# Bias rows written in three DMAs, their tails laid out by GpSimd, and a planner with a shorter cold time

## The chip, the cores and the metric

The kernel runs on one core of one Trainium2 chip. The metric is device time in microseconds (us) of one execution, and the median of several. All times of rows are from one execution recorded by the hardware profiler, counted from its first instruction.

## What is computed

Causal attention with a bias from cumulative sums, whose output is the input of a mixture of experts with dense gates, whose output goes through a two-layer network. The change touches the attention alone:

```python
# q, k, v: (4, 8, 576, 64), s: (4, 8, 576)
scores = scale * np.matmul(q, k.transpose(0, 1, 3, 2))
cum = np.cumsum(np.maximum(s, 0.0), axis=-1)
bias = -(cum[:, :, :, None] - cum[:, :, None, :])
scores = np.where(causal, -1000000000.0, scores + np.minimum(bias, 0.0))
scores = scores - np.max(scores, axis=-1, keepdims=True)
attn = np.exp(scores)
attn = attn / (np.sum(attn, axis=-1, keepdims=True) + 1e-09)
return np.matmul(attn, v).astype(np.float32)
```

Then x is (2304, 512); the mixture has 8 experts of 512 x 1024 x 512, the last network is 512 x 2048 x 512.

## The kernel before

**The attention.** The 32 heads are taken as 16 pairs p = 0 to 15, two heads (h = 0, 1) on the two halves of the 128 partitions. A pair has nine chunks of 128 query rows: four for each head (scores 128, 256, 384 and 512 wide) and a ninth that holds the last 64 rows of both heads (two parts, each 288 wide). For each pair:

- q, k and v are loaded into RB (q and k) and RV (`load_raw`, L403), two DMAs each, one for each head. RB has two places for q and two for k, so pair p's load waits until pair p - 2 has been transposed.
- TensorE transposes q and k (`t_pe`, L477, five each) into a PSUM tile qk, which q and k use in turn. ScalarE and VectorE round q into a high and a low part (L482 to L501, or by way of QF on GpSimd, L506 to L512). k is copied to KF (L515), and GpSimd makes its parts (L519, L533). One copy of each half of q (L490, L492) and of k (L529) goes from SBUF to SBUF by DMA (tile WQ); all of these operands lie in WQ.
- The bias enters as extra rows of the second matmul: `load_bias` (L459, L460) reads the sums of a pair from the DRAM tiles bqd and bkd. For pair 0 they come from SBUF directly.
- A score block is one matmul of the high parts (L543) and one that holds low parts and bias (L544; L548 and L549 for the ninth chunk), into the two banks sc. VectorE masks and takes the maximum (L558, L564, L569), ScalarE the exponential (L576), TensorE transposes (L613, L615) into the two banks tr, ScalarE or VectorE copies these out (L629), and two products with v (`pv0`, `pv1`, L641) fill the tile o. The sums are turned by TensorE (L588), copied (L591), sent through DRAM (L594, L598) and GpSimd scales X by them (L603, L606).

**The bias rows.** The sums over the 32 heads are made once: relu and scan on VectorE (L434, L437), rounding on ScalarE (L440) and remainder on VectorE (L443), into RS0 (64 rows: two parts, two heads of a pair, 16 pairs; 576 columns). `bias_zero` writes zeros to the 64 columns of bqd that a head doesn't use (two DMAs, L447); `bias_write` writes columns 0 to 511 (L450), the 64 tail columns in four pieces whose place depends on the head (L453), and bkd (L454).

**What sets the order.** All of it is put down as tasks (`add`) with an engine, a key, a planned duration and predecessors, and `Plan.order` lays them out: it steps through planned time and gives each engine, among the tasks that are ready, the one of the smallest key. TensorE's durations count twice before a planned time of "cold" thousand ns. The order that comes out is the program; on the chip an engine then runs its own queue strictly in that order and waits by semaphores. So planned durations and predecessors that no data needs change only the order. SP's queue is one of the engines: an issue that waits holds all issues behind it. The first product of the mixture (FA, FB and sc, L314 to L316) and its weights are planned into the end of the attention as well; all that follows has a planner of its own (`flow`).

## Time and profile before

| | us |
|---|---|
| median of 3 runs | 2034.17 (2033.29 to 2038.76) |
| profiled execution | 2032.67 |
| its span, first to last instruction | 2030.8 |
| TensorE busy in the span | 2001.0 (99%) |
| GpSimd, VectorE, ScalarE busy | 1671.3, 1652.8, 904.3 |

The attention takes about the first 210 us of the span. Busy shares are averages over all stages; a stage is read from windows of time, from what each engine waited for, and from the instructions in order of time. A row of the timeline begins with the start and the duration of a group of like instructions; a bracket at its end is the idle time before it and what ended that. SPq rows are DMA issues, whose duration is that of the issue alone.

### The profile page before, as it was taken

How to read it: one execution, taken by the hardware profiler on the slowest of the kernel's cores; microseconds unless marked ns; L12 is line 12 of the kernel's file. 1: busy time of each engine (PE TensorE's matmuls, PEld its weight loads, DVE VectorE, ACT ScalarE, POOL GpSimd, SP SyncE). 2: the span in 40 equal slices, each digit the busy share in tenths (PEclk: the TensorE clock that was granted, in tenths of full speed). 3: DMA queues.
4: the chain of work that ended last, by engine and by line, in shares of the span. 5: the costliest groups of instructions: out<-in, count | busy, mean ns of one | idle time of the engine just before them, and what ended most of it. 6: DMA issues, size and time to landing. Idle time of an engine off the chain costs nothing. (4 is left out here: it accounts for less than half of the span.)

```text
span 2030.8 us, 35314 instructions
## 1 busy us (share of the span) xinstructions
PE 2001.0 (99%) x11939; PEld 1898.0 (93%) x11939; DVE 1652.8 (81%) x2954; ACT 904.3 (45%) x1886; POOL 1671.3 (82%) x1532
## 2 busy tenths in 40 slices
PE   7999999999999999999999999999999999999999
PEld 6777798888889899999999999999999999999999
DVE  5878488888898878888988998989988885766845
ACT  5888433333333344333333344443334345555552
POOL 5778878888888768888887899888878999798783
PEclk9999999999999999999999999999999999999999
DMA  7884888888988777777777788989989877776663
GB/s 160 189 181 120 301 281 291 308 307 300 318 304 308 264 256 253 248 256 247 240 252 250 226 289 302 321 294 309 306 297 308 280 245 242 229 253 216 220 233 116
DMA packets 310241, 524.04 MB, mean 258 GB/s; under 512 B 84044, under 2 KB 197006, under 8 KB 294702
## 3 DMA queue, kind: packets, MB, share of 16 engines
q1 hardware_dynamic: 310024, 521.72, 78.3%
q8 instruction: 95, 1.56, 0.3%
q14 instruction: 84, 0.69, 0.1%
q10 hardware_dynamic: 38, 0.08, 0.0%
HBM read 367.33 MB, written 144.66 MB: 252 GB/s over the span
## 5 line engine op out<-in xcount | busy, mean ns | idle before, releaser
L314 PE MATMUL sc<-XO,WQ 128*128 128x384 f32 x960 | 323.6, 337 | 2.4 <-DVE Uu L1063 1.2
L315 PE MATMUL sc<-XO,WQ 128*128 128x384 f32 x960 | 321.6, 335 | 0.0
L316 PE MATMUL sc<-XO,WQ 128*128 128x384 f32 x960 | 321.5, 335 | 0.0
L1356 ACT CAST WQ<-WQ 128x512 fp32r<-128x512 f32 x172 | 106.9, 622 | 225.4 <-DMA WQ<-w2s 199.9
L1357 DVE TENSOR_TENSOR WQ<-WQ 128x512 fp32r<-128x512 f32 x172 | 183.5, 1068 | 29.1 <-ACT WQ L1356 28.9
L314 PEld LDWEIGHTS sc<-XO,WQ 128*128 128x128 f32 x960 | 180.4, 188 | 9.0 <-DVE Uu L1063 2.1
L315 PEld LDWEIGHTS sc<-XO,WQ 128*128 128x128 f32 x960 | 180.5, 188 | 4.3
L316 PEld LDWEIGHTS sc<-XO,WQ 128*128 128x128 f32 x960 | 180.2, 188 | 0.0
L1063 DVE TENSOR_TENSOR sc<-sc,Uu 128x384 f32<-128x384 f32 x240 | 133.9, 558 | 46.6 <-PE sc L316 45.7
L230 POOL TENSOR_TENSOR WQ<-RB,WQ 128x512 fp32r<-128x512 f32 (+1 forms) x64 | 117.4, 1843 | 58.9 <-ACT WQ L249 54.6
L314 PE MATMUL FA<-XO,WQ 128*128 128x384 f32 x480 | 162.0, 338 | 1.7 <-DVE HB L1091 1.7
L316 PE MATMUL FA<-XO,WQ 128*128 128x384 f32 x480 | 161.1, 336 | 0.3 <-POOL WQ L230 0.3
L315 PE MATMUL FA<-XO,WQ 128*128 128x384 f32 x480 | 161.0, 335 | 0.0
L1337 POOL TENSOR_TENSOR HB<-GG,HB 128x384 fp32r<-128x384 f32 x96 | 110.9, 1158 | 31.0 <-ACT HB L1336 26.3
L1378 DVE TENSOR_TENSOR X<-tr,X 128x384 f32<-128x384 f32 x212 | 115.8, 549 | 23.9 <-PE tr L1372 23.4
L1063 DVE TENSOR_TENSOR Uu<-FB,Up 128x384 f32<-128x384 f32 x120 | 66.2, 551 | 48.0 <-PE FB L316 24.9
L1143 PE MATMUL tr<-WQ,HB 128*128 128x512 f32 x256 | 101.4, 396 | 0.0
L1142 PE MATMUL tr<-WQ,HB 128*128 128x512 f32 x256 | 101.0, 394 | 0.0
L1141 PE MATMUL tr<-WQ,HB 128*128 128x512 f32 x256 | 100.0, 391 | 0.0
L1337 POOL TENSOR_TENSOR HB<-XT,HB 128x384 fp32r<-128x384 f32 x79 | 89.0, 1127 | 12.6 <-ACT HB L1336 12.4
L1063 DVE TENSOR_TENSOR Uu<-sc,Uu 128x384 f32<-128x384 f32 x120 | 65.9, 550 | 39.7 <-PE sc L316 39.4
L314 PEld LDWEIGHTS FA<-XO,WQ 128*128 128x128 f32 x480 | 90.4, 188 | 5.5 <-DVE HB L1091 2.0
(556 smaller groups left out, 7065.6 us busy)
## 6 DMA issues: line engine op xcount, KB each, us to landing
WQ<-w1c SPq DMA_DIRECT2D x88, 1024.0 KB
WQ<-w2d SPq DMA_DIRECT2D x132, 512.0 KB
WQ<-w1c SPq DMA_DIRECT2D x264, 256.0 KB
w1c<-WQ SPq DMA_DIRECT2D x32, 1792.0 KB
WQ<-w2s SPq DMA_DIRECT2D x172, 256.0 KB
RAW<-in_moe_w_dram SPq DMA_DIRECT2D x32, 512.0 KB
w2d<-WQ SPq DMA_DIRECT2D x64, 256.0 KB
w2s<-SS SPq DMA_DIRECT2D x32, 512.0 KB
```

The source lines that it names most:

```text
L230: return lambda: nc.gpsimd.tensor_tensor(out=out, in0=x, in1=y, op=op)
L314: nc.tensor.matmul(t, lhsT=hi, rhs=xh, start=new, stop=False, skip_group_check=on)
L315: nc.tensor.matmul(t, lhsT=hi, rhs=xl, start=False, stop=False, skip_group_check=on)
L316: nc.tensor.matmul(t, lhsT=lo, rhs=xh, start=False, stop=(k == 1), skip_group_check=on)
L1063: TT = lambda out, x, y: (lambda: v.tensor_tensor(out=out, in0=x, in1=y, op=ALU.add))
L1141: nc.tensor.matmul(y, lhsT=hh, rhs=wb[0][:, f], start=(f == 0), stop=False)
L1142: nc.tensor.matmul(y, lhsT=hh, rhs=wb[1][:, f], start=False, stop=False)
L1143: nc.tensor.matmul(y, lhsT=hl, rhs=wb[0][:, f], start=False, stop=(f == 1))
L1337: do(eng, t + 0.02, pgg(W) if eng == "pool" else pq(W), lambda: (nc.gpsimd if eng == "pool" else nc.vector).tensor_tensor(out=OP[k][:, 1], ...
L1356: do("act", t, pa(512), lambda: nc.scalar.copy(hi, lo.bitcast(F32)), [("w2l", k)], [("w2h", k)])
L1357: do(eng, t + 0.05, pgg(512) if eng == "pool" else pd(512), lambda: (nc.gpsimd if eng == "pool" else nc.vector).tensor_tensor(out=lo, in0= ...
L1378: do("dve", t + 0.08, pq(W), lambda: nc.vector.tensor_tensor(out=a, in0=y[:, 0:W], in1=a, op=ALU.add), [yr], [("A", name, s_)])
```

## The change

The tails come from four `affine_select` on GpSimd, which lay the 64 tail columns and the 64 zero columns of each part and head side by side in the second half of a pair's RS1 tile, so that one DMA of 64 x 128 writes them. The zero writes are gone, and bqd is written in two DMAs instead of seven. The third pair's q and k loads no longer have the load of pair 1's v as a predecessor. "cold" goes from 28 to 19, TensorE's planned durations are multiplied by 1.033, and the products with v of the first two pairs have the copies of all nine chunks as predecessors. Lines behind the new function move down by 3. The instructions after the attention come in the same order on every engine.

```diff
-KEYS = {"NE": 11, "PB": 2, "L": 26.0, "bias": 12.3, "Tq": -1.3, "Tk": 6.1, "Tev": -14.1, "Th": 7.8, "top": 17.9, "exp": 14.0, "R": 17.7, "X": 3.9, "hi": -7.3, "lo": 13.7, "cp": "ddaadaaaaddd", "cq": "ddaaddaaaddd", "seq": "012345678", "last": "162308754", "pv": 14.0, "pvh": 33.4, "o": -10.8, "cold": 28.0, "grp": 2, "QP": 1, "w2": 6.0, "w1": 6.0}
+KEYS = {"NE": 11, "PB": 2, "L": 26.0, "bias": 12.3, "Tq": -1.3, "Tk": 6.1, "Tev": -14.1, "Th": 7.8, "top": 17.9, "exp": 14.0, "R": 17.7, "X": 3.9, "hi": -7.3, "lo": 13.7, "cp": "ddaadaaaaddd", "cq": "ddaaddaaaddd", "seq": "012345678", "last": "162308754", "pv": 14.0, "pvh": 33.4, "o": -10.8, "cold": 19, "grp": 2, "QP": 1, "w2": 6.0, "w1": 6.0}
...
-        def bias_zero():
-            for h in range(2):
-                nc.sync.dma_start(out=bqd[:, h, :, S - 64 * h:640 - 64 * h].rearrange("r p n -> p r n"), in_=mask[0:16, 0:128].rearrange("p (r n) -> p r n", r=2))
+        def bias_tail():
+            BT = RS[1][0:64, 0:128]
+            for r in range(2):
+                mine = slice(32 * r, 32 * r + 32)
+                for h in range(2):
+                    nc.gpsimd.affine_select(out=BT[mine, 64 * h:64 * h + 64], in_=BKf[mine, 512:S], pattern=[[0, 64]], compare_op=ALU.is_ge, fill=0.0,
+                                            base=15 - 31 * h, channel_multiplier=2 * h - 1)
 
         def bias_write():
-            nc.sync.dma_start(out=bqd.rearrange("r h p n -> (r h p) n")[:, 0:512], in_=BKf[:, 0:512])
-            for r in range(2):
-                for h in range(2):
-                    nc.sync.dma_start(out=bqd[r, h, :, 512 + 64 * h:S + 64 * h], in_=BKf[32 * r + 16 * h:32 * r + 16 * h + 16, 512:S])
+            rows = bqd.rearrange("r h p n -> (r h p) n")
+            nc.sync.dma_start(out=rows[:, 0:512], in_=BKf[:, 0:512])
+            nc.sync.dma_start(out=rows[:, 512:640], in_=RS[1][0:64, 0:128])
             nc.sync.dma_start(out=bkd.rearrange("r h p n -> (r h p) n"), in_=BKf)
...
-            d[name] = plan.add(eng, key, dur, fn, (), lat)
+            d[name] = plan.add(eng, key, dur * (1.033 if eng == "pe" else 1), fn, (), lat)
...
-        add(("bz",), "sp", -4, 1000, bias_zero, [("setc",), ("bias", 0, 1)], DMA)
-        add(("bw",), "sp", -4, 2500, bias_write, [("cum",), ("bias", 0, 1), ("L", "q", 1)], DMA)
+        add(("bz",), "pool", -25, 1200, bias_tail, [("cum",)])
+        add(("bw",), "sp", -9, 1650, bias_write, [("cum",), ("bz",), ("bias", 0, 1), ("L", "q", 1)], DMA)
...
-                    add(("L", w, p), "sp", b9 - KEY["L"], 950, lambda raw=raw, src=src, p=p: load_raw(raw[p % 2], src, p), [("T", w, p - 2)] + [("L", x, 1) for x in "qkv"], DMA)
+                    add(("L", w, p), "sp", b9 - KEY["L"], 950, lambda raw=raw, src=src, p=p: load_raw(raw[p % 2], src, p), [("T", w, p - 2)] + [("L", x, 1) for x in "qk"], DMA)
...
-                deps = [("cp", b9 + c, a) for c in at_ for a in range(2)] + [("L", "v", p), ("xc", p - 1)] + [("pv0", p, 0)] * part
+                deps = [("cp", b9 + c, a) for c in (range(9) if p < 2 else at_) for a in range(2)] + [("L", "v", p), ("xc", p - 1)] + [("pv0", p, 0)] * part
```

**SP's queue, from the bias tails to the k copy of pair 1.** In_q, in_k and in_v are the loads, RV_100 is v of pair 0, RV_101 v of pair 1; the q and k loads behind v are those of pairs 2 and 3. L490 and L492 (L493 and L495 in the changed kernel) copy q, L529 (L532) copies k. Before:

```order
L453 DMA bqd<-RS_116 16x64 x4
L454 DMA bkd<-RS_116 64x576
L403 DMA RV_100<-in_v_dram 128x5x64 x2
L490 DMA WQ<-WQ 64x576
L403 DMA RV_101<-in_v_dram 128x5x64 x2
L459 DMA WQ<-bqd 2x2x640
L460 DMA WQ<-bkd 2x2x576
L492 DMA WQ<-WQ 64x640
L403 DMA RB<-in_q_dram 128x5x64 x2
L403 DMA RB<-in_k_dram 128x5x64 x2
L529 DMA WQ<-WQ 64x576
```

Now:

```order
L456 DMA bqd<-RS_124 64x128
L457 DMA bkd<-RS_116 64x576
L403 DMA RV_100<-in_v_dram 128x5x64 x2
L403 DMA RB<-in_q_dram 128x5x64 x2
L403 DMA RB<-in_k_dram 128x5x64 x2
L493 DMA WQ<-WQ 64x576
L462 DMA WQ<-bqd 2x2x640
L463 DMA WQ<-bkd 2x2x576
L403 DMA RV_101<-in_v_dram 128x5x64 x2
L403 DMA RB<-in_q_dram 128x5x64 x2
L403 DMA RB<-in_k_dram 128x5x64 x2
L532 DMA WQ<-WQ 64x576
```

The third pair's loads have moved ahead of the q copy and of pair 1's v; the fourth pair's loads, which stood behind the k copy, stand ahead of it, and one q copy has moved behind it.

**TensorE, from pair 0's last transposes into pair 1's scores.** L613 (L616) are transposes of the exponentials, L477 (L480) those of q and k of pair 2, L543 and L544 (L546 and L547) score blocks of pair 1. Before:

```order
L613 MATMUL tr<-ident,EB 128x128 x5
L477 MATMUL qk<-ident,RB 128x128 x5
L613 MATMUL tr<-ident,EB 128x128 x4
L543 MATMUL sc<-WQ 128x128
L544 MATMUL sc<-WQ 128x128
L543 MATMUL sc<-WQ 128x256
L544 MATMUL sc<-WQ 128x256
L613 MATMUL tr<-ident,EAB 128x128 x4
```

Now:

```order
L616 MATMUL tr<-ident,EB 128x128 x2
L480 MATMUL qk<-ident,RB 128x128 x5
L616 MATMUL tr<-ident,EB 128x128 x7
L480 MATMUL qk<-ident,RB 128x128 x5
L616 MATMUL tr<-ident,EAB 128x128 x4
L546 MATMUL sc<-WQ 128x128
L547 MATMUL sc<-WQ 128x128
L546 MATMUL sc<-WQ 128x256
L547 MATMUL sc<-WQ 128x256
```

The q transposes stand three transposes earlier, the k transposes have moved ahead of pair 1's scores, and so has the ninth chunk (EAB).

**TensorE, at the end of the attention.** L314 to L316 into sc are the last product planned ahead of the mixture, L588 (L591) turns the sums, L641 (L644) is the last pair's product. Before:

```order
L316 MATMUL sc<-XO,WQ 128x384
L613 MATMUL tr<-ident,EB 128x128 x3
L588 MATMUL o<-ident,RC 10x128
L314 MATMUL sc<-XO,WQ 128x384
L315 MATMUL sc<-XO,WQ 128x384
L316 MATMUL sc<-XO,WQ 128x384
L314 MATMUL sc<-XO,WQ 128x384
L315 MATMUL sc<-XO,WQ 128x384
L316 MATMUL sc<-XO,WQ 128x384
L641 MATMUL o<-PA_105,RV_101 64x256 x2
```

Now:

```order
L316 MATMUL sc<-XO,WQ 128x384
L616 MATMUL tr<-ident,EB 128x128 x6
L591 MATMUL o<-ident,RC 10x128
L616 MATMUL tr<-ident,EB 128x128
L644 MATMUL o<-PA_105,RV_101 64x256 x2
```

The last transposes and the turning of the sums have moved from between the products to directly ahead of the attention product.

## Rows read from the trace of the kernel before

**Rows 1.** 10 us windows: start:end, length, busy PE, PEld, DVE, ACT, POOL; clock, DMA, GB/s.

```profile
20.00:30.00 10.00, 5.35 (x31) 4.43 (x31) 4.35 (x16) 4.56 (x11) 4.12 (x4) 0.84 0.98 207
...
50.00:60.00 10.00, 10.00 (x82) 7.78 (x82) 8.15 (x30) 8.10 (x23) 7.70 (x11) 1.00 0.76 160
...
220.00:230.00 10.00, 10.00 (x56) 7.32 (x55) 2.66 (x6) 3.92 (x9) 9.24 (x11) 0.93 0.94 343
```

**Rows 2.** TensorE's waits of 0 to 230 us: total, times, longest.

```profile
PE qk L477 <- DMA RB<-in_q_dram: 6.0, 2, 4.3
...
PE sc L544 <- DMA WQ<-WQ: 1.0, 2, 0.6
```

**Rows 3.** The timeline of TensorE around its longest wait.

```profile
20.48 0.74 PE L477 MATMUL qk<-ident,RB 128*128 128x128 f32 x5
...
22.28 0.83 PE L613 MATMUL tr<-ident,EB 128*128 128x128 f32 x5
...
27.45 1.30 PE L477 MATMUL qk<-ident,RB 128*128 128x128 f32 x5 [4.33 <-DMA RB<-in_q_dram]
...
30.00 0.45 PE L544 MATMUL sc<-WQ 68*128 68x128 f32 x1 [0.30 <-issue]
...
36.30 0.44 PE L613 MATMUL tr<-ident,EB 128*128 128x128 f32 x2
```

**Rows 4.** 2 us windows over the same place.

```profile
26.00:28.00 2.00, 0.55 (x3) 0.58 (x4) 0.00 (x0) 0.00 (x0) 0.72 (x1) 0.70 1.14 261
...
30.00:32.00 2.00, 2.00 (x9) 2.00 (x10) 1.64 (x7) 0.86 (x4) 1.32 (x2) 0.50 1.34 228
32.00:34.00 2.00, 2.00 (x10) 1.79 (x9) 0.92 (x3) 1.53 (x5) 0.94 (x1) 0.60 0.50 102
```

**Rows 5.** The timeline of SP's queue: bias writes, v and pair 2's q, k copy, pair 3.

```profile
14.34 0.99 SPq L447 DMA_DIRECT2D bqd<-mask  x2
...
15.37 0.48 SPq L450 DMA_DIRECT2D bqd<-RS  x1
...
15.90 1.98 SPq L453 DMA_DIRECT2D bqd<-RS  x4
...
18.43 1.21 SPq L403 DMA_DIRECT2D RV<-in_v_dram  x2
...
23.68 1.16 SPq L403 DMA_DIRECT2D RB<-in_q_dram  x2
...
26.08 0.52 SPq L529 DMA_DIRECT2D WQ<-WQ  x1
26.70 1.20 SPq L403 DMA_DIRECT2D RB<-in_q_dram  x2
...
29.45 0.56 SPq L529 DMA_DIRECT2D WQ<-WQ  x1
```

**Rows 6.** The timeline of ScalarE and VectorE: the parts of pair 2's q.

```profile
28.83 0.64 ACT L482 ACTIVATE WQ<-qk 64x576 fp32r<-64x576 f32 x1 [4.07 <-issue]
...
30.37 0.75 DVE L498 SCALAR_TENSOR_TENSOR WQ<-qk,WQ 64x576 fp32r<-64x576 f32 x1
```

**Rows 7.** The timeline of TensorE at pair 2's first score block.

```profile
41.31 0.33 PE L544 MATMUL sc<-WQ 68*128 68x128 f32 x1 [0.60 <-DMA WQ<-WQ]
```

**Rows 8.** The timeline: a copy out of tr, and the turning of sums near the end.

```profile
22.17 0.28 DVE L629 COPY PA<-tr 128x128 f32<-128x128 f32 x1
...
194.45 0.28 PE L588 MATMUL o<-ident,RC 128*10 128x128 f32 x1 [0.72 <-DVE RC L585]
```

**Rows 9.** GpSimd and VectorE at the start; last, line 430's two selects (min/median/max).

```profile
6.37 1.34 DVE L437 TENSOR_TENSOR_SCAN EAB<-EB,EAB 32x576 f32<-32x576 f32 x1
...
8.52 0.75 DVE L443 TENSOR_TENSOR RS<-EAB,RS 32x576 fp32r<-32x576 f32 x1
...
10.93 0.67 POOL L519 TENSOR_SCALAR WQ<-KF 64x576 fp32r<-64x576 f32 x1 [2.90 <-DVE KF L515]
...
L430 POOL TENSOR_SCALAR_AFFINE_SELECT mask<-mask x2: 237/688/1138, 6.6 to 7.8; 64x64 f32<-64x64 f32 x2
```

## The prediction

> **What bounds the kernel now.** I read the 10 us windows first. In them TensorE is the engine without gaps: it is busy for all 10 us of 50 to 60, as in most windows of the attention up to 180, and again from 220 to the end [rows 1]. Nothing after the attention is reordered by this change, and TensorE has no idle time there to absorb a later or an earlier start, so the question is only when the attention hands over, and that depends on TensorE's gaps between 0 and 210 us. Second, TensorE's own waits of that stretch: one stands out, for the q rows of a pair, 4.3 us long; besides the first loads there is little else, among it two waits of 1.0 us in all for copies made by DMA (tile WQ) [rows 2]. Third, the timeline around the long wait: TensorE finishes five transposes at 22.28 + 0.83 = 23.11 and starts the q transposes of the third pair (p = 2) only at 27.45, 4.33 us later [rows 3]. Fourth, 2 us windows over the same place: the granted clock falls to one half from about 26.8 (0.70 over 26 to 28 is 1.2 us at 0.5) to about 33.6 (0.60 over 32 to 34), so 2.4 GHz became 1.2 GHz right after that idle time [rows 4]. Last, SP's queue, which issues nearly all DMAs, back to back from 14.34 to 30: the q load that TensorE waits for is issued at 23.68, behind six small bias DMAs that the change removes or merges, and behind the v loads [rows 5].
>
> **SP's queue.** Removed are the two zero writes (0.99) and the four tail writes (1.98); one tail write comes instead, taken at the 0.48 of the main write, so 2.5 us less [rows 5]. The first v load moves from 18.43 to 15.9. The third pair's q and k loads now follow it directly, so q is issued at 15.9 + 1.3 = 17.2 and not 23.68. From issue to use it took 27.45 - 23.68 = 3.8 us [rows 3, 5]: it lands at 21.0, at most 22 with the bias writes and v just ahead of it. TensorE gets there two transposes into the former five, about 22.6. **The 4.33 us wait goes.**
>
> **What is late next.** TensorE then wants the third pair's k transposes, whose PSUM tile is the one q occupies. The q transposes take 0.74 and end at 23.35, ScalarE's rounding 0.64 and VectorE's remainder 0.75 follow [rows 3, 6]: with some 0.2 us for each hand-over TensorE may go on at 25.4, idling about 1 us after the seven transposes put in between. The k transposes (0.74), those of pair 0's last chunk and half a score block bring it to an estimated 27.4. That is the first score block of pair 1, whose second matmul needs the DMA copy of k (source line 529 of the kernel before). It is issued at 26.08 and its matmul starts at 30.00, 3.92 us later [rows 3, 5]; so before the change this wait was hidden right behind the q wait. In the new order the copy stands behind the third and the fourth pair's q and k loads and both v loads. From the first v load to the copy is 26.08 - 18.43 = 7.65 us of queue; one issue leaves it (the q copy, taken at the 0.56 of the k copy and a gap), and the fourth pair's two loads come in front (29.45 - 26.70 = 2.75) [rows 5]. So it is issued at 15.9 + 7.65 - 0.6 + 2.75 = 25.7, only 0.4 us earlier than before, and with 3.92 its matmul starts at 29.6. The bounds for issue to use: 3.1, what the second half of the q load had (issued 0.6 after 23.68), and 5.3, if one more load ahead of it than before costs its transfer (327 680 bytes at the 228 to 261 GB/s that such windows show [rows 4] are 1.4 us). I take 3.92, the same kind of copy in the same crowd; the ends give 28.8 and 31.0.
>
> The Trainium skill (DMA: Bandwidth & Descriptors, "Queues, rings and completion order") says that each DMA engine consumes descriptors in ring order, which speaks against this change: the copy cannot pass the loads now put ahead of it. By that rule the 3.92 or more stands; were the copy able to pass them, 3.1 would be nearer and the sum 0.8 us better. The 3.92 of the copy, against 3.8 for a load issued before it, agrees with the rule.
>
> **From there on.** From that matmul to the first transposes behind the attention product of pair 0 the old kernel takes 36.30 - 30.00 = 6.30 us, 3.6 of them at half clock [rows 3, 4]. The new order has nearly the same instructions there. At full clock the 3.6 would be 1.8 if all of it were TensorE's own work, 6.30 - 1.8 = 4.5 in all; the chain through VectorE that frees the score banks does not halve, so I take 4.7, between 4.5 and 6.3. TensorE reaches that point at 29.6 + 4.7 = 34.3 instead of 36.30: **2.0 us gained**. Both ends together: 28.8 + 4.5 = 33.3 (3.0 gained) and 31.0 + 6.3 = 37.3 (1.0 lost).
>
> **The rest of the attention.** The 1.033 on TensorE's planned durations and the cold time of 19 change no instruction, only the order. Between 37 and 180 TensorE waits twice, 0.60 at 41.31 and 0.45 later, both for such copies [rows 2, 7]. In the new order the two k copies stand ahead of the two reads of the reciprocals; I count the 0.60 as **gained**, with 0 and 1.05 as the ends. The remaining order costs nothing as long as TensorE stays full, which it does there [rows 1]; if that cover is gone, the price is one wait of 0.45 to 0.60 per pair. That the first two pairs' products wait for all nine chunks also costs nothing: in both orders pair 0's product stands behind the last transposes of that pair and two score blocks more, longer than a copy; if that cover is gone, one copy of 0.28 and two hand-overs, 0.7 for each of the two.
>
> At the end, the last transposes of the last pair move behind the two products of the next stage, directly ahead of the attention product. That product must now wait for their copy out of PSUM: 0.28 [rows 8] and two hand-overs of some 0.2 are 0.7 lost, with 0 and 0.8 as ends. The transpose of the sums moves behind one score block and so loses some 0.3 of its wait of 0.72 [rows 8], with 0 and 0.5 as ends. Net **0.4 lost**.
>
> On GpSimd four selects on 32 x 64 are added. GpSimd is idle for 2.90 us before 10.93, waiting for k; the cumulative sums are ready at 8.52 + 0.75 = 9.27, and a 64 x 64 select takes 0.237 when undisturbed [rows 9]. Four with gaps are 1.1 us, from 9.5 to 10.6: hidden, with 0.3 us to spare.
>
> **Sum:** -2.0 - 0.6 + 0.4 = -2.2 us. The profiled execution took 2032.67 us (span 2030.8), so 2030.5; the median of the runs, 2034.17, stands 1.5 above the profiled one, so **2032.0** on that scale. The ends, -3.0 - 1.05 - 0.5 = -4.5 and +1.0 + 0.8 = +1.8, give 2029.7 to 2036.0 for this case. About 0.3% (6.1 us) is what a measurement of this kernel can tell from no change.
>
> **Rivals.**
> A. *The k copy is in time.* If it overtakes the loads and lands by 27, when its scores are due, the next point is reached near 27.0 + 4.7 = 31.7, 4.6 gained; with both copy waits (1.05) and the 0.72 gone and nothing lost at the end, -6.4 or a little more: about 2027.5. For it: the loads ahead of it start 6 us sooner. Against it: DMA is at 0.98 over 20 to 30 [rows 1].
> B. *The clock falls again.* TensorE still idles about 1 us at 24.4 and about 2 us at 27.4. It fell after the 4.33 us of idling, and I cannot read from two levels whether 3 us in pieces suffice. If it falls over the same stretch, 6.3 and not 4.7 is paid: only 0.4 of the 2.0 remain. If it falls over a stretch as long (6.8 us) where TensorE is full, 3.4 is lost against the sum: +1.2. Between 2032.6 and 2035.4; I take 2034.
> C. *Slower: the selects hold GpSimd.* One select of the old kernel took 1.138 instead of 0.237, beside VectorE's scan at 6.37 [rows 9]. Four such are 4.55, to 14.0 and not 10.6, so that the k rounding at 10.93 starts 3.1 late; it decides from 1.4 us in all on. SP's copy of that k, and all issues behind it, shift by 3.1: pair 1's k copy to 28.8, its matmul to 32.7, and after so much idling 6.3 at half clock follow: 39.0 instead of 36.3, with the end +3.1, and up to 3 more if the clock first rises later. 2037 to 2040, say 2038. Against it: at 9.5 VectorE has turned to reading PSUM. The Trainium skill (GPSIMD Engine Reference, "1. Specifications") states that the SBUF interfaces are shared with VectorE and contended by its instructions with two SBUF inputs, which fits the scan and not the two instructions that follow the sums; by it this rival is less likely, and the trace has one select of each kind.
>
> **Chances.** Forecast 0.50, A 0.17, B 0.25, C 0.08. Faster by over 0.3% means under 2028.1: A and a sliver of the forecast, 0.18. Slower means over 2040.3: the upper end of C and orders that cost a wait per pair, 0.07. The same: 0.75. The range leaves out half of A and most of C: 2026.5 to 2037.5.
>
> **What would show it.** The q transposes of pair 2 start near 22.6 without a long wait; the largest wait of TensorE between 20 and 40 is for tile WQ, about 2 us, at its first score block of pair 1 near 29.6; the clock is 1.0 over 28 to 34; the transposes after the first product start near 34.3; the attention's end comes 2 us earlier, and the later stages are as long as before. No such wait, or a stretch of half clock, or selects of over 1 us, show A, B or C; a wait at every pair between 50 and 180 would prove the whole account wrong.

## The result and the profile after

The changed kernel takes **2046.93 us** (median of six runs, 2043.74 to 2048.87) against 2034.79 of six runs of the kernel before: a ratio of **1.0054**, 95% interval 1.0042 to 1.0066, 11 us slower by the ratio (12.1 by the medians), where I forecast 2032.0 and a range up to 2037.5. The profiled execution took 2045.89, its span is 2044.1; against 2030.8 before that is 13.3 us, and the account below is made on these two spans. In the changed kernel the k copy is L532, the write of the reciprocals (the inverted sums of the softmax) to DRAM L597, its reads L601, and GpSimd's scaling of X by them, which the planner calls x_norm, L606.

10 us windows of the changed kernel (the view of [rows 1]):

```profile
30.00:40.00 10.00, 9.88 (x49) 6.89 (x50) 5.08 (x19) 5.01 (x16) 4.15 (x4) 0.66 0.67 159
...
100.00:110.00 10.00, 10.00 (x69) 7.98 (x70) 6.37 (x23) 5.46 (x16) 7.30 (x9) 0.83 1.09 216
...
200.00:210.00 10.00, 6.44 (x30) 4.81 (x27) 4.52 (x14) 5.29 (x14) 9.74 (x10) 0.71 0.00 0
...
220.00:230.00 10.00, 8.60 (x65) 5.82 (x66) 5.28 (x10) 5.05 (x10) 3.48 (x6) 1.00 0.58 176
```

The clock, which was low over 26.8 to 33.6 before, is low at three places now: 0.66 over 30 to 40 takes 3.4 us of full speed away, 0.83 over 100 to 110 takes 1.7, 0.71 over 200 to 210 takes 2.9. The 0.93 that 220 to 230 had before [rows 1] is gone. TensorE's waits between 0 and 230 us (the view of [rows 2]):

```profile
PE sc L547 <- DMA WQ<-WQ: 9.0, 8, 3.4
...
PE sc L546 <- DVE mx L561: 2.7, 2, 1.9
...
PE qk L480 <- DMA RB<-in_q_dram: 1.1, 1, 1.1
```

The long wait for q is gone: 1.1 us in place of 6.0. The waits for the copies of k went from 1.0 us in two to 9.0 in eight. Where the time went can be read from the start of each pair's product with v (first row of tile PA) in the timeline:

| stretch, us | before | after | longer |
|---|---|---|---|
| to the first pair's product with v | 34.42 | 33.18 | -1.2 |
| first to second pair | 11.6 | 14.2 | +2.6 |
| second to sixth pair (four pairs) | 44.2 | 44.1 | -0.1 |
| sixth to seventh pair | 11.1 | 14.8 | +3.8 |
| seventh to fourteenth pair (seven) | 78.0 | 83.1 | +5.0 |
| fourteenth pair to the gates (tile Z) | 30.5 | 35.4 | +4.9 |
| gates to the end | 2021.0 | 2019.3 | -1.7 |

The last line is the half clock that the kernel before has around 220 and the changed one hasn't: 0.90 over 210 to 220 and 0.93 over 220 to 230 are 1.7 us.

**The start.** TensorE and SP's queue of the changed kernel:

```profile
25.51 0.74 PE L480 MATMUL qk<-ident,RB 128*128 128x128 f32 x5 [1.71 <-issue]
...
30.12 0.45 PE L547 MATMUL sc<-WQ 68*128 68x128 f32 x1 [3.38 <-DMA WQ<-WQ]
...
37.16 0.41 PE L616 MATMUL tr<-ident,EB 128*128 128x128 f32 x2
```

```profile
17.26 1.04 SPq L403 DMA_DIRECT2D RB<-in_q_dram  x2
...
24.95 0.82 SPq L532 DMA_DIRECT2D WQ<-WQ  x1
```

The third pair's q is issued at 17.26, the k transposes resume at 25.51, and then TensorE waits 3.38 us for the k copy of pair 1, issued at 24.95 and used 5.17 us later. The clock is half from 30.18 to 37.0, so the transposes behind the first product come at 37.16, not 36.30.

**The pairs in the middle.** SP's queue over one pair, before and after (K load, then reads RS, k copy WQ and write rd):

```profile
78.73 1.28 SPq L403 DMA_DIRECT2D RB<-in_k_dram  x2
80.10 1.87 SPq L492 DMA_DIRECT2D WQ<-WQ  x1
82.02 1.22 SPq L598 DMA_DIRECT2D RS<-rd  x2
83.34 1.18 SPq L529 DMA_DIRECT2D WQ<-WQ  x2
84.62 0.47 SPq L594 DMA_DIRECT2D rd<-RT  x1
```

```profile
78.67 1.14 SPq L403 DMA_DIRECT2D RB<-in_k_dram  x2
79.96 0.53 SPq L495 DMA_DIRECT2D WQ<-WQ  x1
80.54 0.50 SPq L597 DMA_DIRECT2D rd<-RT  x1
81.56 1.22 SPq L532 DMA_DIRECT2D WQ<-WQ  x2
86.14 1.11 SPq L601 DMA_DIRECT2D RS<-rd  x2
...
95.38 0.45 SPq L597 DMA_DIRECT2D rd<-RT  x1
```

Before, a pair's write left right behind the k copies, and its reads a whole pair of loads later. Now the write leaves ahead of the k copies and its reads stand right behind them: SP holds still from 82.78 to 86.14 until the write has landed, with the next pair's loads behind it. The write itself is late, too: the sums turned at 84.40 (TensorE's rows below) are written at 95.38, behind a pair's loads, bias rows and q copies. From the turning of a pair's sums to the issue of their write were 1.3 to 2.8 us in the second to thirteenth pair before; in the third to eleventh they are 7.1 to 11.7 now. SP's and GpSimd's waits between 0 and 230 us, the changed kernel's row first:

```profile
SPq L601 <- DMA rd<-RT: 13.4, 11, 3.3
```

```profile
SPq L598 <- DMA rd<-RT: 1.9, 2, 0.9
```

```profile
POOL X L606 <- DMA RS<-rd: 38.7, 10, 7.0
```

```profile
POOL X L603 <- DMA RS<-rd: 28.6, 13, 3.7
```

GpSimd and TensorE of the changed kernel, a little later:

```profile
82.37 2.91 POOL L536 TENSOR_TENSOR WQ<-KF,WQ 64x576 fp32r<-64x576 f32 x2
90.75 1.28 POOL L606 TENSOR_TENSOR X<-X,RS 128x512 f32<-128x512 f32 x1 [5.47 <-DMA RS<-rd]
```

```profile
79.66 0.87 PE L644 MATMUL o<-PA,RV 128*64 128x256 f32 x8
...
84.40 0.27 PE L591 MATMUL o<-ident,RC 128*10 128x128 f32 x1
...
85.73 0.30 PE L546 MATMUL sc<-WQ 128*128 128x128 f32 x1
86.66 0.30 PE L547 MATMUL sc<-WQ 68*128 68x128 f32 x1 [0.62 <-DMA WQ<-WQ]
...
98.19 0.33 PE L546 MATMUL sc<-WQ 128*128 128x128 f32 x1 [0.39 <-POOL WQ L536]
99.88 0.30 PE L547 MATMUL sc<-WQ 68*128 68x128 f32 x1 [1.36 <-DMA WQ<-WQ]
```

and TensorE before, at the same pair:

```profile
79.18 0.87 PE L641 MATMUL o<-PA,RV 128*64 128x256 f32 x8
...
81.88 0.27 PE L588 MATMUL o<-ident,RC 128*10 128x128 f32 x1
...
86.91 0.33 PE L543 MATMUL sc<-WQ 128*128 128x128 f32 x1
```

x_norm stands on GpSimd ahead of the next pair's q and k parts; it starts 5.47 us after the parts before it are done, and the next k parts and their copy are late by as much less the slack. TensorE's own order takes slack away as well: counted from the product with v, the sums are turned at 4.74 us and not 2.70, and the next pair's first score is due at 6.07 and not 7.73. After the waits of 0.39 and 1.36 us the clock is half over about 101.9 to 105.3. With the 1.7 us which that takes they make 3.45 of the step of 3.8 us.

**The end of the attention.** GpSimd and VectorE before, then GpSimd, VectorE and TensorE of the changed kernel:

```profile
189.13 2.69 POOL L178 TENSOR_TENSOR XO<-XT,XO 128x384 fp32r<-128x384 f32 x2
...
191.85 2.03 DVE L182 TENSOR_TENSOR XT<-X 128x768 f32<-128x768 f32 x1
```

```profile
201.12 1.95 POOL L178 TENSOR_TENSOR XO<-XT,XO 128x384 fp32r<-128x384 f32 x2
...
203.10 2.01 DVE L182 TENSOR_TENSOR XT<-X 128x768 f32<-128x768 f32 x1 [4.46 <-POOL XO L178]
205.03 0.55 DVE L561 CUSTOM_DVE_ANT_0 EB<-sc,mask 128x384 f32<-128x384 f32 x1
```

```profile
203.06 0.66 PE L616 MATMUL tr<-ident,EAB 128*128 128x128 f32 x4 [1.64 <-ACT EAB L579]
...
205.64 0.79 PE L546 MATMUL sc<-WQ 128*128 128x512 f32 x1 [1.92 <-DVE mx L561]
```

What VectorE waits for, a subtraction on GpSimd, ends at 203.07, 4.2 us after the fifteenth pair's product with v starts (198.92); before it ended 1.6 us after (191.82 and 190.22). VectorE's queue has a subtraction into the tile that GpSimd still reads, now ahead of a maximum that it stood behind before, and waits 4.46 us; TensorE runs dry, and the clock is half from about 204.3 to 211.1. This is not the lateness of the middle, carried on: in write_four_sooner, norm_behind_k_parts and sooner_and_behind below most pairs from the third to the fourteenth take 11.0 to 11.3 us, and VectorE waits 4.46 or 4.47 us at this place all the same. In factor_sync_only it is 4.41, in factor_all_but_sync 2.56.

### The profile page after: what moved, and what is told of

The parts are those of the page before. It is cut to its first block, busy times and chain, and to the rows that moved or that the text cites. A ratio compares the mean times of both kernels' runs of the same rounds, so it can differ in the third digit from the quotient of the medians.

```text
span 2044.1 us, 35315 instructions
## 1 busy us (share of the span) xinstructions
PE 2006.8 (98%) x11939; PEld 1902.0 (93%) x11939; DVE 1652.3 (81%) x2954; ACT 902.1 (44%) x1886; POOL 1672.9 (82%) x1536
## 5 line engine op out<-in xcount | busy, mean ns | idle before, releaser
L314 PE MATMUL sc<-XO,WQ 128*128 128x384 f32 x960 | 323.4, 337 | 2.4 <-DVE Uu L1066 1.2
L316 PE MATMUL sc<-XO,WQ 128*128 128x384 f32 x960 | 321.5, 335 | 0.0
L314 PEld LDWEIGHTS sc<-XO,WQ 128*128 128x128 f32 x960 | 180.5, 188 | 8.9 <-DVE Uu L1066 2.3
L316 PEld LDWEIGHTS sc<-XO,WQ 128*128 128x128 f32 x960 | 180.2, 188 | 0.0
L314 PE MATMUL FA<-XO,WQ 128*128 128x384 f32 x480 | 162.4, 338 | 1.2 <-DVE HB L1094 1.0
L316 PE MATMUL FA<-XO,WQ 128*128 128x384 f32 x480 | 161.1, 336 | 0.9 <-POOL WQ L230 0.9
L314 PEld LDWEIGHTS FA<-XO,WQ 128*128 128x128 f32 x480 | 90.5, 189 | 5.4 <-DVE HB L1094 1.4
```

The lines of the kernel that those rows point to most:

```text
L314: nc.tensor.matmul(t, lhsT=hi, rhs=xh, start=new, stop=False, skip_group_check=on)
L316: nc.tensor.matmul(t, lhsT=lo, rhs=xh, start=False, stop=(k == 1), skip_group_check=on)
```

## The experiments

Theory 1: the hold of SP is the price. Theory 2: the start is. Theory 3: TensorE's order (late sums, early scores). Three more came up on the way: the chain through the reciprocals (theory 4), SP's and TensorE's orders that lose only together (theory 6), and the chain whichever link is eased (theory 7). Each ratio is against 11 to 21 runs of the kernel before on the same chip; the medians of these are 2032.4 to 2034.4 us, so the ratios are what to compare.

| run | us | ratio (95%) |
|---|---|---|
| start_alone | 2033.11 | 1.0000 (0.9991 to 1.0009) |
| planner_alone | 2047.52 | 1.0062 (1.0050 to 1.0075) |
| factor_alone | 2047.08 | 1.0066 (1.0054 to 1.0078) |
| reads_behind_write | 2055.85 | 1.0109 (1.0095 to 1.0123) |
| late_in_before | 2050.32 | 1.0088 (1.0074 to 1.0102) |
| factor_sync_only | 2046.52 | 1.0067 (1.0054 to 1.0080) |
| factor_all_but_sync | 2042.65 | 1.0050 (1.0036 to 1.0063) |
| factor_tensor_only | 2063.51 | 1.0154 (1.0141 to 1.0167) |
| reads_four_later | 2075.51 | 1.0209 (1.0195 to 1.0223) |
| write_four_sooner | 2042.12 | 1.0043 (1.0031 to 1.0055) |
| norm_behind_k_parts | 2040.76 | 1.0036 (1.0020 to 1.0052) |
| no_factor | 2041.64 | 1.0042 (1.0030 to 1.0055) |
| write_and_reads_sooner | 2046.42 | 1.0069 (1.0056 to 1.0081) |
| sooner_and_behind | 2041.54 | 1.0045 (1.0032 to 1.0059) |
| planned_landing_4500 | 2036.42 | 1.0018 (1.0009 to 1.0027) |
| bias_alone | 2033.03 | 1.0009 (1.0000 to 1.0018) |
| k_copy_first | 2031.97 | 0.9998 (0.9988 to 1.0009) |
| start_landing_3500 | 2032.65 | 0.9992 (0.9982 to 1.0003) |

**Start or planner.** `start_alone` is the changed kernel with three of its lines undone; `planner_alone` has these three lines alone; `factor_alone` the second.

```diff
-KEYS = {... "cold": 19, ...}
+KEYS = {... "cold": 28.0, ...}
-            d[name] = plan.add(eng, key, dur * (1.033 if eng == "pe" else 1), fn, (), lat)
+            d[name] = plan.add(eng, key, dur, fn, (), lat)
-                deps = [("cp", b9 + c, a) for c in (range(9) if p < 2 else at_) for a in range(2)] + ...
+                deps = [("cp", b9 + c, a) for c in at_ for a in range(2)] + ...
```

> The edits at the start alone (three bias DMAs, the tails on GpSimd, the third pair's loads freed); the planner's numbers as before, so the order from the third pair on is that of before. Theory 1 (the reads of the reciprocals, now right behind the write that they read, hold SyncE for 3.3 us a pair, the DMA queue runs dry, and the k copies come late): none of that is here; the first pair's product with v starts 1 to 2 us earlier and the whole takes 2032 to 2035 us. Theory 2 (the start is the cost: the half clock at 30 to 37 us and what follows from it): 2040 us or more. Theory 3 (TensorE's order: the sums are turned 2 us later and the next pair's first scores come 1.7 us sooner, against the product with v): as theory 1.

> The planner's numbers alone (factor 1.033, cold 19, first pairs' products bound to all copies); bias rows and loads as before. Theories 1 and 3: the whole loss is here, 2045 to 2050 us, and the reads of the reciprocals wait for the write at nearly every pair, some 3 us each. Theory 2: 2034 to 2036 us.

> The kernel before with the factor 1.033 on the planner's durations of TensorE as the only change. It alone puts the reads right behind the write, and the write right ahead of the k copies, from the second write on. Theories 1, 3 and 4: most of the loss, 2042 to 2049 us. If it stays at 2033 to 2036 us, cold time and product bindings make the loss, and the order of SyncE's queue isn't it.

The start edits cost nothing and bring nothing; the planner's numbers cost it all; and the factor, 3.3% on planned durations of TensorE, costs as much by itself. It is enough, but not the only way: see no_factor below. Theory 2 falls.

**One thing moved by hand.** In the next six runs the planner's order is kept but for single tasks. After `order`, the helper takes a task t out of its engine's list and puts it back: `where` tasks later, counted from its own place (u is None) or from that of a named task u. All other engines keep their lists:

```python
...
at = next(i for i, x in enumerate(lst) if x is u)
lst[:] = [x for x in lst if x is not t]
lst.insert(at + where, t)
```

```diff
 # reads_behind_write (from the kernel before)
+plan.moves = [(d["rl", p], d["rw", p], 1) for p in range(NPAIR - 3)]
 # late_in_before (from the kernel before: the write right ahead of the k copies, its reads right behind)
+plan.moves = [m for p in range(1, NPAIR - 3) for m in ((d["rw", p], d["rl", p], 0), (d["rl", p], None, 2))]
 # reads_four_later (from the changed kernel)
+plan.moves = [(d["rl", p], None, 4) for p in range(NPAIR - 6)]
 # write_four_sooner
+plan.moves = [(d["rw", p], None, -4) for p in range(1, NPAIR - 6)]
 # norm_behind_k_parts
+plan.moves = [(d["xn", p], None, 6) for p in range(NPAIR - 7)]
 # write_and_reads_sooner
+plan.moves = [m for p in range(2, NPAIR - 4) for m in ((d["rl", p], None, -2), (d["rw", p], None, -4))]
```

> The kernel before, with one thing moved: the two reads of the reciprocals stand on SyncE's queue right behind the write that they read, in thirteen pairs; every other engine's order is that of before. Theory 1: SyncE is held 3 to 4 us a pair, the DMA queue shows empty stretches, the k copies come late, and the whole takes 2041 to 2048 us. Theory 3: TensorE's order is that of before, so 2034 to 2036 us.

> The kernel before with the changed kernel's order of SyncE's queue put in by hand in twelve pairs: the write moved to right ahead of the k copies, its reads right behind them. All other engines keep the order of before. Theory 4: the write leaves 7 us or more after its sums, the reads wait for it, x_norm and the parts are late: 2041 to 2050 us. Theory 3: TensorE's order is that of before, 2033 to 2036 us.

The changed kernel's place of write and reads on SP, put into the kernel before, costs 18 us, and reads right behind an early write cost 22: SP's order is enough to make the loss. In reads_behind_write GpSimd never waits for the reads, so what costs there is the hold of SP and not x_norm: TensorE waits 10.5 us in nine for copies of k. SP's waits of 0 to 235 us are led by

```profile
SPq L630 <- DMA rd<-RT: 32.9, 15, 3.5
```

The other way round:

> The changed kernel, with one thing moved: the two reads of the reciprocals stand four transfers of the plan later on SyncE's queue (behind the next pair's loads of q and v, bias rows and first q copy), in the first ten pairs; every other engine's order is that of the changed kernel. Theory 1: SyncE waits less than 0.5 us a pair for the write, the k copies are in time again and 8 us or more of the 12 come back: 2034 to 2039 us. Theory 3: TensorE's order is that of the changed kernel, so 2045 to 2048 us.

> The changed kernel, with one thing moved: the write of the reciprocals stands four tasks of the plan earlier on SyncE's queue (ahead of the first q copy, V, second q copy and K), in nine pairs; the reads, and every other engine's order, stay as in the changed kernel. After reads_four_later, theory 1 is cut in two. Theory 1 (the hold of SyncE alone costs). Theory 4 (the chain costs: write, landing, reads, landing, x_norm on GpSimd, which stands ahead of the next pair's q and k parts there, then their copies on SyncE; the write comes 7 to 11 us after the sums are ready because it stands behind q copies, V and K). Theory 3 (TensorE's order). Theories 1 and 4: the reads wait for nothing, x_norm starts some 3 us earlier in its pair, 2033 to 2038 us. Theory 3: 2045 to 2048 us.

> The changed kernel, with one thing moved: on GpSimd the scaling x_norm of a pair stands behind the next q and k parts instead of ahead of them, in the first nine pairs; SyncE's order, with the reads right behind the write, is that of the changed kernel. Theory 4: GpSimd no longer waits for the reads ahead of the parts, the copies are in time, and 6 us or more come back: 2034 to 2041 us, although SyncE is still held some 3 us a pair. Theory 1: the hold is the cost, 2045 to 2048 us. Theory 3: 2045 to 2048 us.

reads_four_later is the most telling miss. SP waits for the write once, 0.2 us, and it is the slowest of all runs. GpSimd's and TensorE's waits of 0 to 235 us there:

```profile
POOL X L638 <- DMA RS<-rd: 66.3, 11, 8.9
```

```profile
PE sc L578 <- POOL WQ L568: 20.4, 8, 4.2
```

The reads come later still, x_norm waits 66.3 us and not 38.7, and the parts behind it are late. So the hold of SP isn't needed for a loss. The chain makes one without it (theory 4): sums, write, landing, reads, landing, x_norm, the next parts, their copies. Which of the two it is in the changed kernel, the next two runs tell. Either link eased brings the loss from 0.54% to 0.43% (write_four_sooner, slower than any theory had it) and 0.36%, with intervals that overlap that of the changed kernel; the traces tell more than the times. In norm_behind_k_parts GpSimd hardly waits for reads, though SP waits for the write nearly as long as in the changed kernel:

```profile
POOL X L638 <- DMA RS<-rd: 12.0, 3, 6.8
```

```profile
SPq L633 <- DMA rd<-RT: 12.9, 12, 2.4
```

Most of its pairs take 11.0 us (11.1 before); what is left is one wait of 2.63 us for a k copy at 109.76 with half clock behind it (a pair of 16.8 us) and the last two pairs. So by this trace the hold costs little in the changed kernel (theory 1 falls there), and x_norm's wait costs. Its runs spread from 2033.59 to 2051.34, where those of the kernel before on that chip spread over 5.8 us; why isn't shown. In write_four_sooner SP waits for the write 2.4 us in three, and the third to the fourteenth pair take 122.5 us, 131.8 in the changed kernel and 122.3 before: the middle's loss is gone in this execution. Lost are the end and 5 us between the second and the third pair, and these my move made: SP stood 3.6 us for the sums of a write that it had put too far forward, and TensorE then waited 3.34 us for a k copy.

> The changed kernel with SyncE's order of before put back by hand in the pairs from the third write to the twelfth: each write four tasks sooner, its reads ahead of the k copies. All other engines keep the changed kernel's order. Theory 4 (the chain write, reads, x_norm, parts on GpSimd): the reads land in time, GpSimd is in time in the last two pairs too, 2033 to 2039 us. Theory 3 (TensorE's order also takes its part: sums turned 2 us later, first scores 1.7 us sooner): 2041 us or more, with waits for k copies at most pairs.

This one is spoilt: at one pair my own move put the write of a later pair, for whose sums SP then waited over 5 us, ahead of K loads and k copies, and TensorE waited 5.61 us there (a pair of 18.5 us). Its time lies in theory 3's range, but TensorE waits for k copies four times and not at most pairs. It decides nothing against theory 4.

**The factor's order, engine by engine.** Here the planner runs twice, without and with the factor, and each engine takes its list from one of the two:

```diff
+        for t in tasks:
+            t[2] *= 1.033 if t[0] == "pe" else 1
+        other = self.order()
+        lists = {e: [t for t in (other if e in self.mixed else tasks) if t[0] == e] for e in ("pe", "act", "dve", "pool", "sp")}
 # factor_sync_only: mixed = ("sp",); factor_tensor_only: ("pe",); factor_all_but_sync: ("pe", "act", "dve", "pool")
```

> The kernel before; SyncE's queue alone in the order that the planner gives with the factor 1.033, the other four engines in the order that it gives without. factor_alone, with all five in the new order, was 13.4 us slower. Theory 4 (the place of write, reads and k copies on SyncE makes the chain late): most of it is here, 2042 us or more. Theory 3 (TensorE's order): 2032 to 2036 us. Theory 6 (the orders only lose together, SyncE's late write and TensorE's early scores): 2036 to 2041 us here and in the two runs beside it.

> The kernel before; SyncE's queue in the order of before, TensorE, ScalarE, VectorE and GpSimd in the order that the planner gives with the factor. Theory 4: 2032 to 2037 us. Theory 3: 2043 us or more. Theory 6: 2036 to 2041 us.

> The kernel before; TensorE alone in the order that the planner gives with the factor, the other four engines in the order of before. Theory 4: 2032 to 2037 us. Theory 3: 2043 us or more, with waits for k copies at most pairs. Theory 6: 2036 to 2041 us.

SP's list alone makes the full loss, 0.67%; the other four lists, with SP's of before, make 0.50%. No theory had that: the two halves don't add up; either, it seems, breaks what fitted. factor_all_but_sync runs at 11.0 to 11.4 us a pair but for three long waits for k copies (2.65, 1.86 and 1.84 us), the first two pairs and the end. factor_tensor_only says little of the changed kernel: TensorE's list no longer fits VectorE's and ScalarE's, and a pair takes 13.3 us.

**Both links eased, and a planner that knows the landing time.** no_factor is the changed kernel without the factor (the second line above); the other edits:

```diff
 # sooner_and_behind
+plan.moves = [(d["rw", p], None, -4) for p in range(1, NPAIR - 5)] + [(d["xn", p], None, 6) for p in range(NPAIR - 5)]
 # planned_landing_4500 (changed kernel); start_landing_3500 (start_alone) with 3500.0
-        DMA = 2000.0
+        DMA = 4500.0
```

> The changed kernel without the factor: write, k copies, then q and v loads, and only then the reads (no wait for the write, as in reads_four_later), x_norm ahead of the parts. Theory 1: SyncE isn't held by the reads, 2033 to 2038 us. Theory 4: the reads are issued 2 us later than the write's landing would allow, x_norm and the parts are as late as in the changed kernel or later: 2045 us or more.

> The changed kernel with both single moves that gave some of the loss back: the write of the reciprocals four tasks sooner on SyncE (ten pairs) and the scaling x_norm behind the next q and k parts on GpSimd (eleven pairs). Theory 7 (the loss is the chain through the reciprocals, whichever link is eased, and what remains of it after one ease is single waits for a k copy, each followed by half the clock, and the end of the attention): the steady pairs take 11.0 to 11.1 us each as before, only the last two pairs stay some 4 us longer: 2035 to 2039 us. If TensorE's early first scores are late on their own account: 2041 us or more, with waits for k copies at several pairs.

> The changed kernel with the planner's landing time of every transfer at 4500 ns, about what the traces show from issue to use (rw to reads 3.3 us of waiting after 1.7 of other issues, k copy 3.9 to 4.6), in place of 2000. The planner then puts Q and V between write and reads by itself. Theory 7: the reads wait for nothing, but their landing is no earlier; where the planner also moves x_norm and the parts it may fit: 2034 to 2042 us, with the last two pairs as the largest part. If the planned time of transfers doesn't matter: 2044 to 2048 us.

> The start edits alone (as start_alone, the planner's other numbers as before) with the planned landing time of every transfer at 3500 ns in place of 2000. On SyncE the planner keeps q, v and k loads between write and reads, as before, in most pairs. Theory 7: no wait for the write, the pairs take 11.0 to 11.2 us each, and what the start gains reaches the end of the attention: 2030 to 2035 us, at best 2 us under the kernel before. If any replanned order costs by itself, as all of the others did: 2036 us or more.

no_factor met neither range: its reads hardly wait (1.8 us in two) and its pairs take 11.3 us (55.2 to 179.9 in eleven), but its last two pairs 36.4 and not 30.5. It differs from start_alone, which costs nothing, by the cold time and the bound products alone: these lose 0.42% without the factor. sooner_and_behind ended at the edge of its second range, for the reason that write_four_sooner had: the middle is as before but for one wait of 3.17 us at 56.53, behind SP's stand of 3.6 us for sums, with half clock after it, and one of 0.67 us later; and the end is as in the changed kernel. planned_landing_4500 brings the loss from 0.54% to 0.18%, with intervals that don't touch and no list touched by hand. Its SP queue over a pair, and a window:

```profile
79.11 0.95 SPq L403 DMA_DIRECT2D RB<-in_k_dram  x2
80.72 0.31 SPq L597 DMA_DIRECT2D rd<-RT  x1
81.12 0.94 SPq L403 DMA_DIRECT2D RB<-in_q_dram  x2
82.14 1.12 SPq L532 DMA_DIRECT2D WQ<-WQ  x2
83.36 1.18 SPq L403 DMA_DIRECT2D RV<-in_v_dram  x2
84.63 1.21 SPq L601 DMA_DIRECT2D RS<-rd  x2
```

```profile
100.00:120.00 20.00, 20.00 (x156) 15.74 (x151) 16.08 (x56) 15.21 (x45) 14.38 (x16) 1.00 0.94 200
```

Loads fill the time in which the write lands, and TensorE has no wait for a copy between 40 and 170. Yet a pair takes 11.46 us (53.28 to 179.33 in eleven), not 11.1, with TensorE busy for all of it. What makes the pair longer isn't settled. Every engine's order is a new one here, and one value was tried, so that the landing time is what helped, and not a luckier order, is argued and not shown. start_landing_3500, which keeps before's sequence on SP in most pairs, is at 0.9992 (0.9982 to 1.0003): no difference that can be measured, and neither of the runs that came out below before is shown to beat it.

**What the start is worth.** bias_alone is start_alone with the third pair's q and k loads behind all three loads of pair 1 again; k_copy_first is start_alone with one move, the k copy ahead of the fourth pair's q and k loads:

```diff
 # bias_alone
-    ... [("T", w, p - 2)] + [("L", x, 1) for x in "qk"], DMA)
+    ... [("T", w, p - 2)] + [("L", x, 1) for x in "qkv"], DMA)
 # k_copy_first
+plan.moves = [(d["kd", 1, 0], d["L", "q", 3], 0)]
```

> The kernel before with the bias edit alone (three DMAs, tails on GpSimd); the third pair's loads still stand behind V. By the prediction's account of the start the queue is 2.5 us shorter, the q wait of 4.33 us shrinks to some 2, nothing new stands ahead of the k copy, and 1.5 to 2.5 us are gained: 2031 to 2032 us. If the start's gain is lost on the way through the attention (as in start_alone, where it was 1 us at the fourth pair and nothing at the end): 2033 to 2035 us.

> The start edits alone (as start_alone), with the first k copy of the second pair moved ahead of the second V's successors, the third pair's q and k loads. In start_alone TensorE waits 5.62 us for this copy, issued at 26.15 behind those loads and landed at 30.5. Issued at 23.0 instead it lands near 26.5; the wait falls below 2 us and the clock stays full or nearly so. If what the start gains reaches the end: 2029 to 2031 us. If it is lost later: 2033 to 2034 us.

bias_alone gains nothing: the wait for q that was 4.33 us is 1.27, but the fourth pair's loads stand ahead of the k copy there too. It is issued at 26.20 (26.08 before), TensorE waits 5.11 us for it, and the first product with v starts at 35.36 and not 34.42. TensorE at the first score block of pair 1, in start_alone and in k_copy_first:

```profile
30.57 0.45 PE L547 MATMUL sc<-WQ 68*128 68x128 f32 x1 [5.62 <-DMA WQ<-WQ]
```

```profile
26.29 0.33 PE L579 MATMUL sc<-WQ 68*128 68x128 f32 x1 [1.48 <-DMA WQ<-WQ]
```

Issued at 22.97 and not 26.15, the copy is used after 3.32 us and not 4.42, and the wait falls from 5.62 to 1.48. The gates start at 207.81, 2.0 us before those of the kernel before; at 1224 us the lead is still 2.2 us, by 1484 it is gone, behind waits of TensorE for VectorE (1.6 and 0.8 us between 1260 and 1440, where before has 0.5 and 0.3). So even a start that does gain doesn't reach the end in this execution.

## Why the prediction was wrong

The step that failed is the one in "The rest of the attention": **"The remaining order costs nothing as long as TensorE stays full, which it does there"**. That TensorE is full is a result of the order, not a cover for changing it. [Rows 1] show that nothing waits, not by how little. The slack stands elsewhere: from the issue of the k copy at 83.34 to its use at 87.08 in the kernel before are 3.7 us, about what such a copy takes (3.3 to 5.2 in these traces). I gave the price of a lost cover as "one wait of 0.45 to 0.60 per pair" and a chance of a few per cent; the waits in the middle were 0.4 to 1.4 us at seven pairs, 6.1 in all, and the half clock behind them (1.7), which I had not priced, and the end of the attention (4.9, where I had 0.4) cost as much again.

Point by point:
- **"The two k copies stand ahead of the two reads of the reciprocals; I count the 0.60 as gained."** The same rows of the order held the loss: the reads had come right behind their write. I read them for the copies and not for what the reads now wait for, nor for x_norm on GpSimd behind them. This term turned from -0.6 to +8.7 (-0.1 + 3.8 + 5.0).
- **SP's queue**: right. q issued at 17.26 (17.2 forecast), the 4.33 us wait gone.
- **What is late next**: right in place, short in size. The k transposes at 25.51 (25.4), the copy's matmul at 30.12 (29.6); 5.17 us from issue to use, near the upper bound of 5.3 and not the 3.92 I took. By the Trainium skill (DMA: Bandwidth & Descriptors, "Queues, rings and completion order") the descriptors on each DMA engine are consumed in ring order. The runs agree: the copy was used 4.42 us after its issue with the fourth pair's loads ahead of it (start_alone), 3.32 with them behind it (k_copy_first).
- **"At full clock ... I take 4.7"**: wrong, rival B. The clock was half from 30.18, right behind the 3.38 us wait, and the stretch took 7.04 us (30.12 to 37.16). In the kernel before it fell at 26.8, still within the wait that ended at 27.45, and not behind it as I had read. The 2.0 us gained became 0.9 lost at that point [rows 3].
- **The start's gain reaches the end**: in start_alone it is 0.3 us at the fourth pair (67.8 against 68.1), 0.6 at the fourteenth (178.79 against 179.35) and none at the gates (210.05 against 209.82). Even without the new order the sum would have been 0, not -2.2. In the changed kernel 2.6 us more are lost between the first two pairs, half clock up to 37 among them.
- **The cold time and the first two products bound to nine chunks, "also costs nothing"**: with the start edits alone beside them they cost 0.42% (no_factor). Which of the two does isn't separated.
- **The end, 0.4 lost**: 4.9 lost. Ahead of the last product stand 0.43 us of waiting, of the 0.7 I had; what I had not seen is VectorE's wait of 4.46 us for GpSimd a pair earlier, which comes with the order at the end and not from the middle.
- **The selects**: right. Four in 1.40 us, from 8.19 to 9.59, and GpSimd then idles 1.10 us for k [rows 9]. Rival C did not occur.
- **Rivals**: none was this one. (B's lower end is 2033.6 by its own terms, not 2032.6: 1.6 us of the 2.0 are lost.) The text had named the sign of it ("a wait at every pair between 50 and 180 would prove the whole account wrong") and left it almost no chance.

Shown by times: the planner's factor alone makes a loss as large as the whole, SP's list of it alone too, and cold time with bound products lose without it; the chain loses without a hold of SP (reads_four_later), and a hold without the chain (reads_behind_write); the order that is planned with a landing time of 4.5 us loses 0.18%. Shown by one trace each, and not clear of the noise in the times: that the write's place or x_norm's alone gives the middle's loss back. Not shown: how the loss divides between SP's late chain and TensorE's early scores, since lists of single engines don't fit together otherwise, and what in the order at the end makes its 4.9 us.

## What to carry to other kernels

Where a planner orders queues, a change of planned durations is a change of every queue: compare the orders engine by engine over one steady period, and ask of each issue that waits what it waits for and what is queued behind it, also on the engine that uses the data (here GpSimd). An engine without gaps tells that the slack is enough, not how large it is: read that from issue to use of the copies that feed it. A planner should have the landing times that the trace shows, here 3.3 to 5.6 us where it had 2: with 4.5 the same change cost 0.18% and not 0.54%. And the middle and the end of a pipeline lose separately: an order that is good in one can be bad in the other.

## What the runs showed of the hardware

The Trainium skill (DMA: Bandwidth & Descriptors, "Anatomy of one DMA — SWDGE (gpsimd) path") gives some 2.0 us as the fixed cost of one DMA on GpSimd's path. That is also the planner's number, for transfers that SP issues. Here a 5 KB write issued at 80.54 had landed for its reads at 86.14, 5.6 us later, and k copies were used 3.3 to 5.2 us after their issue, while that queue's packets took 74.7% of the 16 DMA engines' time (46 to 180 us). A short wait can cost twice its length: 0.39 and 1.36 us at 98 to 100 us were followed by half clock from about 101.9 to 105.3, another 1.7 us. It need not: waits of 2.65, 1.86 and 1.84 us in factor_all_but_sync, ending at 88.79, 112.90 and 170.27, left the granted clock at 1.00 over 86 to 100, 110 to 124 and 168 to 182. And a list without such waits is not the fastest: 11.46 us a pair in planned_landing_4500 with TensorE busy throughout, against 11.1.
